# Scores of the later query blocks as plain fp32 products, the two token halves of a block in the two halves of the array's columns

## The chip, the core and the metric

The kernel runs on one core of a Trainium2 chip. The metric is the device time of one execution in microseconds (us). The engines are named as in the profile: PE is TensorE (PEld its weight loads), DVE is VectorE, ACT is ScalarE, POOL is GpSimd, SP is the engine that issues most transfers.

## What is computed

Attention through 49 agents and two feed-forward layers behind it, all in fp32, for 12480 tokens of 128 channels:

```python
a2k = sm(agents, k)              # sm(a, b): softmax of a @ b.T / sqrt(128)
agent_v = a2k @ v                # 49 x 128
q2a = sm(q, agents)              # 12480 x 49: the scores that the change touches
x = q2a @ agent_v
h = np.maximum(x @ w_in, 0.0)    # 128 -> 2048
x = (s * (h * h) + b) @ w_out    # 2048 -> 128
h = np.maximum(x @ w_in2, 0.0)
out = (h * h) @ w_out2
```

## The kernel before

Everything runs on one core with an order written out by hand: within each engine, instructions stand as the Python code issues them. A first part reads keys and values, makes the agents' results and folds them with the first weights into a matrix `M` (49 agents twice, in 128 rows). The main loop then goes over 25 blocks of tokens, 23 of 512 and 2 of 352, in eight steps a block. A step `st` of block `t` issues one pair of 128-row chunks of the first layer up (`up1`, 4 products), of the second layer up for an earlier block (`up2`, 6), and of both layers down (`down`, 6 each). Accuracy is kept by splitting fp32 values into a high and a low part of type float32r: a product is then two or three float32r products that add up in PSUM.

Between these products stands the query work of the next block, one piece at each of some steps: scores (`q_scores` for blocks 0 to 2, `q_scores_T` for the later ones, at step 1), transposing back (`q_back`, step 2), exponential, normalising, and `q_stack`, which makes the block's operand `X`. For blocks from `DIRECT` = 3 on, the queries arrive with channels on the partitions: by a transposing transfer, or every fourth block (`TURN`) by a plain one and a transpose on DVE (`q_turn`, tile `qt`). They are loaded three blocks ahead into three buffers `q_raw`.

For these later blocks the scores work in parts. `q_transpose` copies the queries to a high part `qh` (ACT), `q_low` makes the low part `ql` at the next block's step 0 (DVE). The weights `aS` hold the agents' high parts in columns 0 to 48 and their low parts in columns 64 to 112. `q_scores_T` multiplies low and high queries with `aS`, all 512 tokens at a time, into the PSUM tile `ps_sT`. Two ACT copies and two DVE additions then bring agent high and low rows together into `sT`, where the first 256 tokens of the block lie on partitions 0 to 48 and the second 256 on 64 to 112. `q_back` turns that by two transposes (`ps_b`).

Of the kernel before, what the change touches and what calls it, by code (L numbers as in the profile page):

```python
# [9 lines left out]
F32 = mybir.dt.float32  # L10
F32R = mybir.dt.float32r
# [3 lines left out]
ALU = mybir.AluOpType  # L15
AX = mybir.AxisListType

P = 128
# [15 lines left out]
DIRECT = 3  # L34
# [11 lines left out]
def tile_agent_attention_two_moe(  # L46
# [14 lines left out]
    nc = tc.nc  # L61
    _, N, C = q.shape
    NA = agents.shape[1]
# [4 lines left out]
    GAP = 64  # L68
    KS = GAP + NA
# [13 lines left out]
    blocks, left = [], N  # L83
# [13 lines left out]
    const = ctx.enter_context(tc.tile_pool(name="const", bufs=1))  # L97
    qp = ctx.enter_context(tc.tile_pool(name="qp", bufs=2))
    qs = ctx.enter_context(tc.tile_pool(name="qs", bufs=2))
# [5 lines left out]
    def small(name):  # L105

        flip[0] = (flip[0] + 1) % (flip[1] + 1)
        return ps_m.tile([P, 512], F32, tag=f"m{flip[0]}", name=name)
# [5 lines left out]
    wo2 = [const.tile([P, NCH, C], F32R, name=f"wo2{x}") for x in "hl"]  # L114
    stacks = [const.tile([P, 4, GAP], F32, name=f"stack{i}") for i in range(2)]
    sTs = [const.tile([KS, 256], F32, name=f"sT{i}") for i in range(2)]
    aS = const.tile([P, P], F32R, name="aS")
    av = [const.tile([P, P], F32R, name=f"av{x}") for x in "hl"]
    ones_r = const.tile([P, P], F32R, name="ones_r")
    Xs = [const.tile([P, 512], F32R, name=f"X{i}") for i in range(2)]  # L120
    aT = const.tile([P, GAP], F32, name="aT")
# [1 line left out]
    b_sb = const.tile([P, 1], F32, name="b_sb")  # L123
    y1_bias = const.tile([P, 1], F32, name="y1_bias")
    const.tile([P, 120], F32, name="apart0")
    halves = (0, slice(0, NA)), (1, slice(GAP, KS))

    def split(dst, src, eng_lo, copy=nc.vector.tensor_copy):

# [4 lines left out]
    q_raw, qT, q_sT, q_e, q_st, X = {}, {}, {}, {}, {}, {}  # L134
# [35 lines left out]
    def q_transpose(t):  # L170
        _, p, j = blocks[t]
        n = p * j
        raw = q_raw.pop(t)
        if t < DIRECT:
            ps = small("ps_q")
            for i in range(j):
                nc.tensor.transpose(
                    out=ps[:, i * p:(i + 1) * p], in_=raw[:p, i * C:(i + 1) * C], identity=ident[:p, :p]
                )
            qT[t] = qs.tile([P, 512], F32, tag="qh", name="qT")  # L180
            nc.scalar.copy(qT[t][:, :n], ps[:, :n])
        else:
            hi = qs.tile([P, 512], F32R, tag="qh", name="qh")
            lo = qs.tile([P, 512], F32R, tag="ql", name="ql")
            nc.scalar.copy(hi[:, :n], raw[:, :n])
            qT[t] = (hi, lo, raw)

    def q_low(t):
        _, p, j = blocks[t]
        n = p * j  # L190
        hi, lo, raw = qT[t]
        nc.vector.tensor_tensor(out=lo[:, :n], in0=raw[:, :n], in1=hi[:, :n].bitcast(F32), op=ALU.subtract)

    def q_shift(t, sc):
        _, p, j = blocks[t]
# [16 lines left out]
    def q_scores_T(t):  # L212

        _, p, j = blocks[t]
        n = p * j
        x = qT.pop(t)
        ps = small("ps_sT")
        for z in (1, 0):
            nc.tensor.matmul(out=ps[:, :n], lhsT=aS, rhs=x[z][:, :n], start=(z == 1), stop=(z == 0))  # L219
        sT = sTs[t % 2]  # L220
        for h, to in halves:
            nc.scalar.copy(sT[to, :2 * p], ps[:NA, 2 * p * h:2 * p * (h + 1)])
        for h, to in halves:
            nc.vector.tensor_tensor(
                out=sT[to, :2 * p], in0=ps[GAP:KS, 2 * p * h:2 * p * (h + 1)], in1=sT[to, :2 * p], op=ALU.add
            )
        q_sT[t] = sT

    def q_back(t):
# [9 lines left out]
    def q_exp(t):  # L239
        _, p, j = blocks[t]  # L240
        e = q_e[t]
        nc.scalar.activation(e[:p, :j], e[:p, :j], AF.Exp, scale=SCALE)
# [137 lines left out]
    def finish(n):  # L380

        while undone[0] > n:
            fill(1)

    def m_piece(i):

        sl = slice(i * WC, (i + 1) * WC)
        ps = small("ps_M")
        for z, (x, w) in enumerate(((av[0], wi[1]), (av[1], wi[0]), (av[0], wi[0]))):
            nc.tensor.matmul(out=ps, lhsT=x, rhs=w[:, sl], start=(z == 0), stop=(z == 2))  # L390
        split((M[0][:, sl], M[1][:, sl]), ps, nc.vector, nc.scalar.copy)

    with tc.manual_schedule():

        with tc.tile_pool(name="pre", bufs=1) as pre, tc.tile_pool(name="kp", bufs=2) as kp:
# [23 lines left out]
            nc.gpsimd.memset(aT, 0.0)  # L419
            for x in v_buf:  # L420
                nc.gpsimd.memset(x[:, :, C:], 1.0)
            for x in [aS] + av:
                nc.gpsimd.memset(x.bitcast(F32), 0.0)
            for x in stacks + sTs:
                nc.gpsimd.memset(x, 0.0)
# [9 lines left out]
            ps = small("ps_w")  # L435
            for i in range(16):
                nc.tensor.transpose(out=ps[:, :P], in_=ident, identity=ident)
            ps = small("ps_a")
            nc.tensor.transpose(out=ps[:, :NA], in_=ag, identity=ident[:NA, :NA])
            nc.vector.tensor_copy(aT[:, :NA], ps[:, :NA])  # L440
            nc.vector.tensor_copy(aS[:, :NA], aT[:, :NA])
            nc.vector.tensor_tensor(out=aS[:, GAP:KS], in0=aT[:, :NA], in1=aS[:, :NA].bitcast(F32), op=ALU.subtract)
            mxa = pre.tile([P, 8, NA], F32, name="mxa")

            def k_transpose(g):
# [43 lines left out]
            mxk = pre.tile([P, NA], F32, name="mxk")  # L489
            nc.vector.reduce_max(mxk, mxa.rearrange("p j n -> p n j"), axis=AX.X)  # L490
            q_transpose(0)
            fill(FILL_T)
            ps = small("ps_mt")
# [7 lines left out]
            ps = small("ps_mb")  # L501
# [12 lines left out]
            def set_bias():  # L514
                x = qs.tile([P, 512], F32, tag="ql", name="cs")
                nc.vector.tensor_tensor(
                    out=x.rearrange("p (m c) -> p m c", c=C),
                    in0=ps_cs.rearrange("p (m c) -> p m c", c=C),
                    in1=ident.rearrange("p (m c) -> p m c", m=1).to_broadcast([P, 512 // C, C]),
                    op=ALU.mult,  # L520
                )
                nc.vector.reduce_sum(y1_bias, x, axis=AX.X)
                nc.vector.tensor_mul(y1_bias, y1_bias, b_sb)
# [13 lines left out]
            for g, (_, p, j) in enumerate(kblocks):  # L537
# [6 lines left out]
                for i in range(j):  # L544
                    nc.tensor.matmul(  # L545
                        out=ps_av[:NA, :C + 1],
                        lhsT=S[:p, t0[g] + i],
                        rhs=vs[g][:p, i],
                        start=(g == 0 and i == 0),
                        stop=(g == NG - 1 and i == j - 1),  # L550
# [11 lines left out]
            ps = small("ps_avT")  # L562
# [5 lines left out]
            for c0 in (0, GAP):  # L568
                nc.vector.tensor_tensor(
                    out=av[1][:, c0:c0 + NA], in0=ps[:, :NA], in1=av[0][:, c0:c0 + NA].bitcast(F32), op=ALU.subtract  # L570
# [10 lines left out]
        NB = len(blocks)  # L581
# [12 lines left out]
        def up1(t, i):  # L594
            n = blocks[t][1] * blocks[t][2]
            ps = ps_h.tile([P, 2, 512], F32, tag="h", name="ps_h1")
            for c in range(2):
                sl = slice((2 * i + c) * P, (2 * i + c + 1) * P)
                for z in (1, 0):
                    nc.tensor.matmul(out=ps[:, c, :n], lhsT=M[z][:, sl], rhs=X[t], start=(z == 1), stop=(z == 0))  # L600
            G1[t, i] = hidden(ps, n, 1, nc.scalar.copy if t * NPR + i in HI_ACT else nc.vector.tensor_copy)
# [50 lines left out]
        for st in range(total + L2 + LAG + 1):  # L652
            t, i = divmod(st, NPR)
            if t + 1 < NB and i == QS[2]:
                q_exp(t + 1)
            if st == NPR:
                set_bias()
            for first, left in ((L2, 2 * NW), (L2 + LAG, NW)):
                c, r = divmod(st - first, WC // (2 * P))
                if r == 0 and 0 <= c < NW:  # L660
                    finish(left - 1 - c)
            if st in M_AT:
                m_piece(2 + M_AT.index(st))
            if st < len(FILL_L):
                fill(FILL_L[st])
            if i == 0 and DIRECT <= t + 1 < NB:
                q_low(t + 1)
            if t < NB:
                up1(t, i)
                if i == 0:  # L670
                    for u, far in ((t + 2, t + 2 < DIRECT), (t + 3, DIRECT <= t + 3 < NB)):
                        if far:
                            q_load(u)
                if t + 1 < NB:
                    if t + 2 < NB and i == NPR - 2:
                        q_turn(t + 2)
                    elif t + 2 < NB and i == NPR - 1:
                        q_transpose(t + 2)
                    if i == QS[0]:
                        (q_scores if t + 1 < DIRECT else q_scores_T)(t + 1)  # L680
                    elif i == QS[1] and t + 1 >= DIRECT:
                        q_back(t + 1)
                    elif i == QS[3]:
                        q_norm(t + 1)
                    elif i == QS[4]:
                        q_stack(t + 1)
            t, i = divmod(st - L2, NPR)
            if 0 <= t < NB:
                up2(t, i)
            t, i = divmod(st - LAG, NPR)  # L690
            if 0 <= t < NB:
                down(t, i, wo, G1, py1, "y1")
                if i == NPR - 1:
                    y1_done(t)
            t, i = divmod(st - L2 - LAG, NPR)
            if 0 <= t < NB:
                down(t, i, wo2, G2, py2, "y2")
                if i == NPR - 1:
                    y2_done(t)
# [30 lines left out]
```

## Time and profile before

| what | value |
|---|---|
| median of three runs | 1091.5 us (1089.89 to 1091.57) |
| the profiled execution's own time | 1091.76 us |
| its span, first to last instruction | 1089.8 us |
| PE, DVE, ACT busy in the span | 1073.8, 933.2, 932.9 us |
| mean granted TensorE clock | 0.993 |

The span is what the trace covers; the execution's own time has 2.0 us more around it. Busy time of PE is the time in which at least one matmul record is open; records are longer than the distance between them, since matmuls are pipelined. So the distance of starts tells what a product costs in a row of products.

### The profile page before, as it was taken

The numbers are of one execution on the slowest core, as the hardware profiler recorded it, in microseconds if no ns is written. First come the engines' busy times: TensorE is split into PE (matmuls) and PEld (weight loads), VectorE is DVE, ScalarE is ACT, GpSimd is POOL, SyncE is SP. The second block draws the span as 40 slices with busy tenths as digits, with TensorE's granted clock in tenths as the row PEclk, the third lists the DMA queues.
The fourth block names the chain that finished last, engine by engine and source line by source line (L and its number), as shares of the span: only waits on it lengthen the run. The fifth ranks groups of instructions, "written<-read, shape, count | busy, mean of one in ns | idle before, by whom it ended". The sixth has DMA issues, their size and how long they took to land.

```text
span 1089.8 us, 13795 instructions
## 1 busy us (share of the span) xinstructions
PE 1073.8 (99%) x5105; PEld 903.8 (83%) x5105; DVE 933.2 (86%) x1278; ACT 932.9 (86%) x1081; POOL 12.5 (1%) x36
## 2 busy tenths in 40 slices
PE   9998999999999999999999999999999999999998
PEld 9886788888888888888888888888888888888897
DVE  6888888888888888888888888888888888888876
ACT  6659989889889889889889888888888888888886
POOL 2010000000000000000000000000000000000000
PEclk9899999999999999999999999999999999999999
DMA  9999989992499991499992599991599990000000
GB/s 340 300 173 11 14 4 17 16 8 21 13 8 17 16 7 21 13 7 16 17 7 20 14 7 16 17 7 20 13 8 16 17 5 17 11 2 10 11 10 14
DMA packets 1110795, 34.86 MB, mean 32 GB/s; under 512 B 1092983, under 2 KB 1107144, under 8 KB 1110728
## 3 DMA queue, kind: packets, MB, share of 16 engines
q1 hardware_dynamic: 1107888, 27.58, 99.4%
q0 software_dynamic: 1728, 6.29, 1.8%
q8 instruction: 40, 0.66, 0.4%
q14 instruction: 27, 0.22, 0.1%
q10 hardware_dynamic: 1112, 0.12, 0.1%
HBM read 27.58 MB, written 6.39 MB: 31 GB/s over the span
## 4 chain that ended last, share of the span: by engine, by line
PE 92%; DMA 3%; ACT 1%; DVE 1%; SPq 1%; issue 1%; DVEq 0%
PE ps_y L626 48%; PE ps_h L610 25%; PE ps_h L600 16%; PE ps_av L545 2%; DMA kraw<-in_k_dram 2%; DMA q_raw<-in_q_dram 1%; PE ps_sT L219 1%; SPq L154 1%; ACT r L589 1%; PE ps_x L265 0%; ACT r L590 0%; PE ps_b L234 0%; DVE gl L131 0%; PE ps_cs L512 0%; PE ps_M L390 0%
## 5 line engine op out<-in xcount | busy, mean ns | idle before, releaser
L131 DVE TENSOR_TENSOR gl<-r,gh 128x1024 fp32r<-128x1024 f32 (+2 forms) x402 | 479.8, 1194 | 15.9 <-ACT gh L130 2.3
L589 ACT ACTIVATE r<-ps_h 128x1024 f32<-128x1024 f32 (+2 forms) x402 | 400.4, 996 | 87.7 <-PE ps_h L600 78.3
L590 ACT ACTIVATE r<-r 128x1024 f32<-128x1024 f32 (+2 forms) x402 | 416.5, 1036 | 12.8
L130 DVE CAST gh<-r 128x1024 fp32r<-128x1024 f32 (+1 forms) x397 | 267.4, 674 | 113.6 <-ACT r L590 108.1
L610 PE MATMUL ps_h<-yh,wi2l 128*128 128x512 f32 (+1 forms) x400 | 157.8, 394 | 0.2 <-ACT r L589 0.2
L600 PE MATMUL ps_h<-X,Ml 128*128 128x512 f32 (+1 forms) x400 | 154.1, 385 | 2.1 <-DVE X L276 1.3
L626 PE MATMUL ps_y<-gh,wol 128*128 128x512 f32 (+1 forms) x400 | 154.1, 385 | 1.0 <-ACT y L634 1.0
L626 PE MATMUL ps_y<-gl,woh 128*128 128x512 f32 (+1 forms) x400 | 153.8, 385 | 0.6 <-DVE gl L131 0.6
L600 PE MATMUL ps_h<-X,Mh 128*128 128x512 f32 (+1 forms) x400 | 154.0, 385 | 0.0
L610 PE MATMUL ps_h<-yh,wi2h 128*128 128x512 f32 (+1 forms) x400 | 153.9, 385 | 0.0
L610 PE MATMUL ps_h<-yl,wi2h 128*128 128x512 f32 (+1 forms) x400 | 153.9, 385 | 0.0
L626 PE MATMUL ps_y<-gl,wo2h 128*128 128x512 f32 (+1 forms) x400 | 153.7, 384 | 0.1
L626 PE MATMUL ps_y<-gh,wo2l 128*128 128x512 f32 (+1 forms) x400 | 153.6, 384 | 0.0
L626 PE MATMUL ps_y<-gh,wo2h 128*128 128x512 f32 (+1 forms) x400 | 153.6, 384 | 0.0
L626 PE MATMUL ps_y<-gh,woh 128*128 128x512 f32 (+1 forms) x400 | 153.6, 384 | 0.0
L600 PEld LDWEIGHTS ps_h<-X,Ml 128*128 128x128 f32 x400 | 75.4, 188 | 17.8 <-issue 2.9
L626 PEld LDWEIGHTS ps_y<-gh,wol 128*128 128x128 f32 x400 | 75.3, 188 | 16.3 <-ACT y L634 1.5
L626 PEld LDWEIGHTS ps_y<-gl,woh 128*128 128x128 f32 x400 | 75.3, 188 | 15.7 <-DVE gl L131 1.0
L600 PEld LDWEIGHTS ps_h<-X,Mh 128*128 128x128 f32 x400 | 75.4, 188 | 15.0
L610 PEld LDWEIGHTS ps_h<-yh,wi2h 128*128 128x128 f32 x400 | 75.1, 188 | 14.7
L626 PEld LDWEIGHTS ps_y<-gl,wo2h 128*128 128x128 f32 x400 | 75.2, 188 | 14.5 <-DVE gl L131 0.6
L626 PEld LDWEIGHTS ps_y<-gh,woh 128*128 128x128 f32 x400 | 75.2, 188 | 14.4
(122 smaller groups left out, 887.3 us busy)
## 6 DMA issues: line engine op xcount, KB each, us to landing
kraw<-in_k_dram SPq DMA_DIRECT2D x12, 512.0 KB, 12.0
v<-in_v_dram SPq DMA_DIRECT2D x12, 512.0 KB, 7.9
out_dram<-o SPq DMA_DIRECT2D x92, 64.0 KB, 1.9
q_raw<-in_q_dram SPq DMA_DIRECT2D x18, 256.0 KB, 41.3
raw<-in_moe_w_out_dram POOLq DMA_DIRECT2D x8, 512.0 KB, 7.3
raw<-in_moe_w_in_dram SPq DMA_DIRECT2D x4, 512.0 KB, 7.7
raw<-in_moe_w_in_dram POOLq DMA_DIRECT2D x4, 512.0 KB, 6.9
q_raw<-in_q_dram SPq DMA_DIRECT2D x20, 64.0 KB, 2.3
```

The source lines that it names most:

```text
L130: copy(dst[0], src)
L131: eng_lo.tensor_tensor(out=dst[1], in0=src, in1=dst[0].bitcast(F32), op=ALU.subtract)
L154: nc.sync.dma_start(out=q_raw[t].rearrange("p (j c) -> p j c", c=C)[:p, :j], in_=tokens_of(q, t))
L219: nc.tensor.matmul(out=ps[:, :n], lhsT=aS, rhs=x[z][:, :n], start=(z == 1), stop=(z == 0))
L545: nc.tensor.matmul(out=ps_av[:NA, :C + 1], lhsT=S[:p, t0[g] + i], rhs=vs[g][:p, i], start=(g == 0 and i == 0), stop=(g == NG - 1 and i == ...
L589: nc.scalar.activation(r[:, c, :n], ps[:, c, :n], AF.Relu)
L590: nc.scalar.activation(r[:, c, :n], r[:, c, :n], AF.Square)
L600: nc.tensor.matmul(out=ps[:, c, :n], lhsT=M[z][:, sl], rhs=X[t], start=(z == 1), stop=(z == 0))
L610: nc.tensor.matmul(out=ps[:, c, :n], lhsT=w[:, sl], rhs=y[:, :n], start=(z == 0), stop=(z == 2))
L626: nc.tensor.matmul(out=py[t][:, :n], lhsT=wz[:, m], rhs=g[:, c, :n], start=(m == 0 and z == 0), stop=(m == NCH - 1 and z == 2),)
```

## The change

`q_scores_T` multiplies the fp32 queries as they are, with the fp32 agents `aT` (64 columns, of which 49 are used and the rest zero), in two products of 256 tokens, one per half of the block. The result of the first goes to partitions 0 to 63 of `ps_sT`, that of the second to partitions 64 to 127, so to the lower and the upper half of the array's columns. One ACT copy of 113 partitions brings both into `sT`. The parts `qh`, `ql` and `aS`, with `q_low` and the additions, go.

```diff
@@ const
-    aS = const.tile([P, P], F32R, name="aS")
...
-    halves = (0, slice(0, NA)), (1, slice(GAP, KS))
@@ q_transpose
-            hi = qs.tile([P, 512], F32R, tag="qh", name="qh")
-            lo = qs.tile([P, 512], F32R, tag="ql", name="ql")
-            nc.scalar.copy(hi[:, :n], raw[:, :n])
-            qT[t] = (hi, lo, raw)
-
-    def q_low(t):
-        _, p, j = blocks[t]
-        n = p * j
-        hi, lo, raw = qT[t]
-        nc.vector.tensor_tensor(out=lo[:, :n], in0=raw[:, :n], in1=hi[:, :n].bitcast(F32), op=ALU.subtract)
+            qT[t] = raw
@@ q_scores_T
-        n = p * j
+        n = 2 * p
         x = qT.pop(t)
         ps = small("ps_sT")
-        for z in (1, 0):
-            nc.tensor.matmul(out=ps[:, :n], lhsT=aS, rhs=x[z][:, :n], start=(z == 1), stop=(z == 0))
+        for h in range(2):
+            nc.tensor.matmul(
+                out=ps[GAP * h:GAP * (h + 1), :n], lhsT=aT, rhs=x[:, n * h:n * (h + 1)], start=True, stop=True
+            )
         sT = sTs[t % 2]
-        for h, to in halves:
-            nc.scalar.copy(sT[to, :2 * p], ps[:NA, 2 * p * h:2 * p * (h + 1)])
-        for h, to in halves:
-            nc.vector.tensor_tensor(
-                out=sT[to, :2 * p], in0=ps[GAP:KS, 2 * p * h:2 * p * (h + 1)], in1=sT[to, :2 * p], op=ALU.add
-            )
+        nc.scalar.copy(sT[:, :n], ps[:KS, :n])
@@ first part
-            for x in [aS] + av:
+            for x in av:
...
-            nc.vector.tensor_copy(aS[:, :NA], aT[:, :NA])
-            nc.vector.tensor_tensor(out=aS[:, GAP:KS], in0=aT[:, :NA], in1=aS[:, :NA].bitcast(F32), op=ALU.subtract)
@@ main loop
-            if i == 0 and DIRECT <= t + 1 < NB:
-                q_low(t + 1)
```

On PE, at step 1 of block 2, the scores of block 3 stand between that step's `up1` and `up2`. Before (a row is line, operation, result <- operands, shape of the result):

```order
L600 MATMUL ps_h_1414<-X_90,Ml 128x512
L600 MATMUL ps_h_1414<-X_90,Mh 128x512
L219 MATMUL ps_sT<-ql,aS 128x512
L219 MATMUL ps_sT<-qh,aS 128x512
L610 MATMUL ps_h_1433<-yh,wi2l 128x512
L610 MATMUL ps_h_1433<-yl,wi2h 128x512
```

In the changed kernel the same place on PE reads:

```order
L584 MATMUL ps_h_1406<-X_89,Ml 128x512
L584 MATMUL ps_h_1406<-X_89,Mh 128x512
L208 MATMUL ps_sT<-q_raw,aT 64x256 x2
L594 MATMUL ps_h_1422<-yh,wi2l 128x512
L594 MATMUL ps_h_1422<-yl,wi2h 128x512
```

Two products of 64 rows by 256 columns have taken the place of two of 128 by 512, with the same neighbours; nothing else moves on PE.

On ACT, the copies out of `ps_sT` stand at the end of the same step, between two blocks' hidden activations. Before:

```order
L589 ACTIVATE r<-ps_h_2823 128x1024
L590 ACTIVATE r<-r 128x1024
L222 COPY sT_85<-ps_sT 49x256 x2
L589 ACTIVATE r<-ps_h_2842 128x1024
L590 ACTIVATE r<-r 128x1024
```

In the changed kernel:

```order
L573 ACTIVATE r<-ps_h_2787 128x1024
L574 ACTIVATE r<-r 128x1024
L212 COPY sT_85<-ps_sT 113x256
L573 ACTIVATE r<-ps_h_2803 128x1024
L574 ACTIVATE r<-r 128x1024
```

One copy of 113 partitions stands for two of 49. The cast L185 to `qh`, two steps earlier on ACT, and on DVE the subtraction L192 and the two additions L224 are gone without anything in their place.

## Rows read from the trace of the kernel before

**Rows 1.** The page, part 1: busy time, share of the span, instructions.
```profile
span 1089.8 us, 13795 instructions
...
PE 1073.8 (99%) x5105; PEld 903.8 (83%) x5105; DVE 933.2 (86%) x1278; ACT 932.9 (86%) x1081; POOL 12.5 (1%) x36
```

**Rows 2.** Windows: length, busy time by engine, granted clock (PEclk), DMA share, GB/s.
```profile
core 0: us, PE busy (x) PEld busy (x) DVE busy (x) ACT busy (x) POOL busy (x), PEclk, DMA share, GB/s
75.00:140.00 65.00, 58.14 (x253) 46.35 (x254) 58.91 (x88) 59.75 (x69) 0.00 (x0) 0.97 1.68 11
140.00:1000.00 860.00, 860.00 (x3838) 712.05 (x3837) 747.60 (x956) 759.70 (x846) 0.00 (x0) 1.00 1.07 13
1045.00:1089.80 44.80, 39.99 (x243) 38.94 (x241) 30.71 (x49) 30.61 (x44) 0.00 (x0) 0.98 0.09 15
```

**Rows 3.** Timeline of PE, scores of block 3: start, length (us), line, product.
```profile
139.58 0.39 PE L600 MATMUL ps_h<-X,Mh 128*128 128x512 f32 x1
139.80 0.39 PE L219 MATMUL ps_sT<-ql,aS 128*128 128x512 f32 x1
140.03 0.39 PE L219 MATMUL ps_sT<-qh,aS 128*128 128x512 f32 x1
140.26 0.39 PE L610 MATMUL ps_h<-yh,wi2l 128*128 128x512 f32 x1
...
144.34 0.39 PE L600 MATMUL ps_h<-X,Ml 128*128 128x512 f32 x1
...
145.25 0.36 PE L234 MATMUL ps_b<-ident,sT 113*128 113x113 f32 x2
```

**Rows 4.** Tile ps_sT: count, ns min/median/max, first and last start, forms.
```profile
L222 ACT COPY sT<-ps_sT x44: 281/350/366, 142.0 to 998.5; 49x256 f32<-49x256 f32 x40, 49x176 f32<-49x176 f32 x4
L224 DVE TENSOR_TENSOR sT<-ps_sT,sT x44: 335/422/429, 144.0 to 1000.1; 49x256 f32<-49x256 f32 x40, 49x176 f32<-49x176 f32 x4
...
L219 PE MATMUL ps_sT<-ql,aS x22: 319/389/389, 139.8 to 996.6; 128*128 128x512 f32 x20, 128*128 128x352 f32 x2
```

**Rows 5.** Timeline of PE in the first part: runs of plain fp32 work.
```profile
9.78 1.04 PE L450 MATMUL ps_k<-ident,kraw 128*128 128x128 f32 x8
10.66 1.90 PE L460 MATMUL ps_ks<-aT,kT 128*128 128x64 f32 x16
```

**Rows 6.** Line L545, the agents' values: 98 plain fp32 products.
```profile
L545 PE MATMUL ps_av<-v,S x196: 271/273/454, 46.2 to 70.5; 128*49 128x129 f32 x192, 96*49 96x129 f32 x4
```

**Rows 7.** Timeline of PE, the longest run of L545.
```profile
54.20 16.58 PE L545 MATMUL ps_av<-v,S 128*49 128x129 f32 x148
```

**Rows 8.** Timeline of PE, a narrow window: two transposes between passes of L545.
```profile
53.37 0.49 PE L545 MATMUL ps_av<-v,S 128*49 128x129 f32 x3
53.80 0.47 PE L265 MATMUL ps_x<-ident,stack 128*113 128x128 f32 x2
54.20 0.53 PE L545 MATMUL ps_av<-v,S 128*49 128x129 f32 x3
```

**Rows 9.** Timeline of PE, from L545 to float32r products of 512 columns.
```profile
70.29 0.49 PE L545 MATMUL ps_av<-v,S 96*49 96x129 f32 x3
...
71.05 0.40 PE L512 MATMUL ps_cs<-wol,ones_r 128*128 128x512 f32 x1
```

**Rows 10.** Timeline of PE's weight loads at the same place; in brackets the idle time.
```profile
70.71 0.19 PEld L512 LDWEIGHTS ps_cs<-woh,ones_r 128*128 128x128 f32 x1 [0.19 <-issue]
```

**Rows 11.** Timeline of PE's weight loads, scores of block 3.
```profile
139.58 0.19 PEld L219 LDWEIGHTS ps_sT<-ql,aS 128*128 128x128 f32 x1
```

**Rows 12.** Tile q_raw, columns as in Rows 4.
```profile
L158 SPq DMA_DIRECT2D q_raw<-in_q_dram x16: 633/634/1161, 61.9 to 860.6; - x16
L185 ACT CAST qh<-q_raw x16: 467/604/607, 132.3 to 948.6; 128x512 fp32r<-128x512 f32 x15, 128x352 fp32r<-128x352 f32 x1
L192 DVE TENSOR_TENSOR ql<-q_raw,qh x16: 517/684/687, 136.9 to 953.0; 128x512 fp32r<-128x512 f32 x15, 128x352 fp32r<-128x352 f32 x1
...
L167 DVE STREAM_TRANSPOSE qt<-q_raw x6: 540/704/705, 169.6 to 986.1; 128x512 f32<-128x512 f32 x5, 128x352 f32<-128x352 f32 x1
```

**Rows 13.** The page, part 6: the transposing transfers, KB each, us to landing.
```profile
q_raw<-in_q_dram SPq DMA_DIRECT2D x18, 256.0 KB, 41.3
```

## The prediction, made before the changed kernel was run

> **What bounds the kernel now.** I first read the page's busy times: TensorE (PE) is busy 1073.8 us of a span of 1089.8, VectorE (DVE) and ScalarE (ACT) 933 each [rows 1]. An average over stages does not say where a saving counts, so the table by windows comes next: from 140 us to 1000 us PE is busy in every microsecond and at the full granted clock (1.00, the level of 2.4 GHz), while DVE and ACT have about an eighth of the time free; PE lacks 6.9 us in the window from 75 to 140, and 4.8 us in the last 45 [rows 2].
>
> Busy need not mean useful, since records of matmuls overlap. So the third view is PE's timeline around a changed place. Products of 512 columns start at 139.58 and, 21 later, at 144.34: 4.76 / 21 = 0.2267 us apart, and the two score products of L219 stand in this row at the same distance [rows 3]. From the first L219 at 139.8 to the last at 996.6 lie 21 blocks [rows 4]: about 40.8 us each. A block has 22 x 8 products of the two layers and 2 of scores, 178 x 0.2267 = 40.35, and four transposes, at 0.11 each (a run of eight of 128 columns lasts 1.04 with a last record of 0.27: 0.77 / 7 [rows 5]) 0.44: together 40.79. So nothing is lost to waits: in this stage the kernel is the sum of what PE issues. A slot more or less per block goes into the time in full; work on DVE and ACT does not, as long as they keep up.
>
> **The change, part by part.** It concerns 22 of the 25 blocks (3 to 24), 20 of them of 512 tokens and 2 of 352 [rows 4].
>
> *Removed from PE:* two products of 512 columns, 2 x 0.2267 = 0.4534 us; in the two short blocks two of 352, in proportion 2 x 0.156 = 0.312.
>
> *Added to PE:* two plain fp32 products, each with 64 score columns in the array and 256 tokens passing. How such a product is carried out is seen at L545, also fp32, with 49 score columns in the array: its 98 products have 196 records [rows 6], so each is two passes. A run of 148 passes over 129 columns lasts 16.58, the last record 0.27 [rows 7]: 16.31 / 147 = 0.111 us a pass, 0.86 ns a column. (The fp32r products take 0.2267 / 512 = 0.44 ns: a plain pass costs twice that, and there are two.) A pass of 256 columns is thus 0.220 us, one of 176 is 0.151. There are four passes: end to end 0.881, against 0.4534 removed. What rows of this kernel do not show is whether passes of the two halves, which use different columns of the array and different output partitions, can run beside each other: wherever plain products follow each other here they use the same columns. The bounds are four passes in a row (0.881), and the halves fully side by side (two passes, 0.440).
>
> *The change of shape.* L545 differs from its neighbours in that its results fill fewer than half of the array's columns (128*49), as the new products do; L265 and L512 use more than half. Where three of L545's passes are followed by two transposes and three passes again, the first starts at 53.37 and the last ends at 54.73, so starts at 54.46: 1.09 us, where five distances of 0.111 and two of 0.11 make 0.775. Two crossings, out and in, cost 0.315 [rows 8]. The way out alone: the last L545 starts at 70.29 + 0.49 - 0.27 = 70.51, the second L512 at 71.05, which is 0.54 instead of 0.111 + 0.227: 0.20 [rows 9]; so the way in costs 0.115. The load for the first L512 does not run ahead there: PE's weight loads are 0.19 idle and it starts with its product [rows 9, 10], while in the main loop each load starts with the product before, as that of L219 at 139.58 [rows 3, 11]. The new products lie between products with 128 columns in the array, so each block pays one way in and one out, 0.315. The Trainium skill, "TensorEngine Tiling (Array Packing)", section Key Properties, says that changing the tiling mode, not just the tile, drains the engine; the trace agrees with 0.315 us for two changes, and by that rule nothing is paid between the halves.
>
> *The middle load.* If the second half may start beside the first, its first weights are loaded only when the first half's second pass has begun [rows 11]. A load of 128 columns takes 0.108 (16 passes of L460, too short to cover their loads, last 1.90 less 0.275, over 15 [rows 5]), one of 64 half of that, 0.054.
>
> *Removed from ACT:* the cast L185, 0.604, and one of two copies of 0.350; the one that is left has 113 partitions instead of 49, so it costs between 0.350 and 0.700 (no row has this shape; I take 0.350, since the columns are 256 as before). *From DVE:* L192, 0.684, and two L224 of 0.422 [rows 4, 12]. That is some 0.95 of ACT and 1.53 of DVE a block, on engines that have free time [rows 2]: nothing for the time. If their cover were gone these would be the most they could give, 1.5 x 22 = 34 us, but PE has no gap in that stage to close. The two DVE operations that build aS at about 6 us lie outside it as well; the gaps of PE before 140 and after 1045 us fall into the first blocks and the last layer, where the change has no work. I cost all of this at nothing.
>
> *Waits.* The first pass no longer waits for L192, only for the transfer of the queries or, every fourth block, for DVE's transpose L167, whose first is at 169.6, 11 us ahead of its block's scores (139.8 + 40.8). A raw block is held until the second half is done, 3 us longer (139.8 instead of 136.9), so its buffer's next transfer may start 3 us later. The last transposing transfers are issued at 860.6 and take 41.3, and are read only from 948.6 on [rows 12, 13]: hidden. The transposes L234, at 145.25, now follow a single ACT copy instead of two copies and two additions of 0.422 from 144.0 on [rows 3, 4]: also no wait.
>
> **Sum.** I take the order of the passes as kept, so that only the middle two, the first half's second and the second half's first, can meet: three passes in a row and the middle load. Per full block 3 x 0.220 + 0.054 + 0.315 - 0.4534 = +0.576; per short block 3 x 0.151 + 0.054 + 0.315 - 0.312 = +0.51. 20 x 0.576 + 2 x 0.51 = +12.5 us. The profiled execution's own time is 1091.76 (its span 1089.8 and 2.0 around it), the median of the timed runs 1091.5; on this median the changed kernel takes 1104.0 us, 1.1% more.
>
> **The rivals.**
> A, *no overlap at all*: four passes in a row. 0.881 + 0.315 - 0.4534 = +0.742, short blocks 0.606 + 0.315 - 0.312 = +0.61: 14.8 + 1.2 = +16.0, 1107.5 us. For it: every row of plain products has them one behind the other. Against it: each of these rows has a reason, the same columns.
> The Trainium skill, "TensorE: Matmul & The Clock Gate", section Part 3 on packing small matmuls, has products in different column groups run concurrently, in program order, with 2.38 times the speed measured for three; no run here shows it yet. By the rows alone the price would be A's +16.0, by that rule the sum above, or C if the passes pair up completely.
> C, *halves fully side by side*: two passes, 0.440 + 0.315 - 0.4534 = +0.302, short 0.302 + 0.315 - 0.312 = +0.30: +6.6, 1098.1 us. Against it: the second pass of half 0 stands before both of half 1 in the queue.
> D, *not slower*: the halves side by side and the change of shape hidden, 0.440 - 0.4534 = -0.013 a block: 1091.2 us, no change. It decides only if a block's extra stays under 0.10 us (2.2 / 22), and the 0.315 of the crossings [rows 8] speaks against it. A gain of more than 0.2% would need PE to get shorter: nothing in the profile gives that.
>
> **How the numbers follow.** The main case has 0.47, A 0.31, C 0.14, D 0.05; 0.03 is left for what I have not seen. The range from 1098 to 1109 holds the main case, A with its crossings 0.07 dearer a block than measured, and reaches C, whose value lies on its lower edge. About 0.2% (2.2 us) is what a measurement of this kernel can tell from no change: all cases but D are slower, 0.93; D gives 0.05 for the same; 0.02 is left for faster.
>
> **What the profile after would show.** PE still busy in every microsecond from 140 to 1000. At each place of the scores: four records with 256 columns, two for each half; the start of the third says which case holds: beside or just behind the second (main case, some 0.05 after it), 0.22 after it (A), with the first (C). From the last product before to the first after, some 1.2 us instead of 0.68. The period of a block goes from 40.8 to 41.4 (A 41.6, C 41.1). ACT and DVE lose some 21 and 34 us of busy time, and their idle time before the hidden activations grows. I would be wrong if PE showed gaps in front of the scores (the transfers late), or if the passes took another time a column in the upper half of the array than L545's do in the lower.

## The result and the profile after

The changed kernel takes 1099.69 us (median of six, 1099.21 to 1100.23) against 1091.33 (1089.89 to 1091.65) in the same comparison: ratio 1.0076, 95% interval 1.0066 to 1.0087, so 8.4 us slower, as forecast in sign, with about two thirds of the forecast size.

The page, part 1, and the same windows as before, the last one moved with the span:

```profile
span 1097.8 us, 13770 instructions
...
PE 1082.2 (99%) x5149; PEld 898.4 (82%) x5149; DVE 905.4 (82%) x1210; ACT 915.8 (83%) x1037; POOL 12.3 (1%) x35
```

```profile
75.00:140.00 65.00, 58.30 (x254) 46.17 (x256) 58.96 (x88) 59.63 (x69) 0.00 (x0) 0.97 1.67 11
140.00:1000.00 860.00, 860.00 (x3845) 700.32 (x3842) 714.89 (x885) 736.59 (x795) 0.00 (x0) 1.00 1.07 13
1045.00:1097.00 52.00, 47.99 (x285) 46.20 (x284) 37.65 (x58) 37.47 (x53) 0.00 (x0) 0.99 0.07 13
```

PE is still busy in every microsecond of the main loop at the same granted clock. Over the whole span DVE has 27.8 us less to do and ACT 17.1 [rows 1] (in the window the differences are larger, 32.7 and 23.1 [rows 2], also because a little less of the loop fits into the same 860 us), and the loop is longer all the same: the time is made on PE. The tile `ps_sT`, columns as in rows 4:

```profile
L208 PE MATMUL ps_sT<-q_raw,aT x64: 312/379/430, 139.7 to 963.9; 128*64 128x256 f32 x60, 128*64 128x176 f32 x4
...
L208 PE MATMUL ps_sT<-qt,aT x24: 313/379/431, 180.9 to 1004.5; 128*64 128x256 f32 x20, 128*64 128x176 f32 x4
L212 ACT COPY sT<-ps_sT x22: 284/356/356, 141.9 to 1005.9; 113x256 f32<-113x256 f32 x20, 113x176 f32<-113x176 f32 x2
```

There are 88 records, four for each of 22 blocks. In PE's timeline the first block's scores start at 139.73, the last one's at 1004.30:

```profile
1004.30 0.52 PE L208 MATMUL ps_sT<-qt,aT 128*64 128x176 f32 x4
```

That makes 864.57 / 21 = 41.17 us a block, where it was 40.80 [rows 4]. The 0.37 times 22 are 8.1 us, practically the whole difference. Where they lie is seen in PE's timeline at the place of rows 3:

```profile
139.41 0.39 PE L584 MATMUL ps_h<-X,Mh 128*128 128x512 f32 x1
139.73 0.65 PE L208 MATMUL ps_sT<-q_raw,aT 128*64 128x256 f32 x4
140.32 0.50 PE L594 MATMUL ps_h<-yh,wi2l 128*128 128x512 f32 x1
140.65 0.39 PE L594 MATMUL ps_h<-yl,wi2h 128*128 128x512 f32 x1
...
141.81 0.39 PE L610 MATMUL ps_y<-gh,wol 128*128 128x512 f32 x1
```

Four records fit into 0.65 us. With a last record of 0.38 the last one starts at 140.00, 0.27 after the first; four passes one behind the other would put three distances of 0.22 between them. So the halves run together. Around them every distance is longer than it should be: 0.32 from the last L584 to the first L208 (0.227 between full products), 0.27 from the first passes to the second (0.22), 0.32 from the second passes to L594 (0.22), 0.33 from the first L594 to the second (0.227). PE's weight loads of the same place show what goes with it:

```profile
139.73 0.20 PEld L208 LDWEIGHTS ps_sT<-q_raw,aT 128*64 128x64 f32 x4 [0.35 <-issue]
140.31 0.19 PEld L594 LDWEIGHTS ps_h<-yh,wi2l 128*128 128x128 f32 x1 [0.39 <-issue]
```

Before, each load started with the product ahead of it [rows 11]. Here, at both ends of the visit, the loads stand idle for 0.35 and 0.39 us and start only with their own product, as in rows 10.

### The profile page after: what moved, and what is told of

The parts are those of the page before. It is cut to its first block, busy times and chain, and to the rows that moved or that the text cites. A ratio compares the mean times of both kernels' runs of the same rounds, so it can differ in the third digit from the quotient of the medians.

```text
span 1097.8 us, 13770 instructions
## 1 busy us (share of the span) xinstructions
PE 1082.2 (99%) x5149; PEld 898.4 (82%) x5149; DVE 905.4 (82%) x1210; ACT 915.8 (83%) x1037; POOL 12.3 (1%) x35
## 4 chain that ended last, share of the span: by engine, by line
PE 92%; DMA 3%; ACT 2%; DVE 1%; issue 1%; SPq 0%; DVEq 0%; ACTq 0%
PE ps_y L610 47%; PE ps_h L594 25%; PE ps_h L584 15%; PE ps_av L529 2%; DMA kraw<-in_k_dram 2%; DMA q_raw<-in_q_dram 1%; PE ps_sT L208 1%; ACT r L573 1%; ACT r L574 1%; PE ps_x L251 0%; DVE gl L129 0%; PE ps_b L220 0%; PE ps_cs L496 0%; PE ps_q L175 0%; PE ps_s L198 0%
## 5 line engine op out<-in xcount | busy, mean ns | idle before, releaser
L594 PE MATMUL ps_h<-yh,wi2l 128*128 128x512 f32 (+1 forms) x400 | 160.6, 401 | 0.2 <-ACT r L573 0.2
L584 PE MATMUL ps_h<-X,Ml 128*128 128x512 f32 (+1 forms) x400 | 154.1, 385 | 2.1 <-DVE X L262 1.3
L594 PE MATMUL ps_h<-yh,wi2h 128*128 128x512 f32 (+1 forms) x400 | 154.3, 386 | 0.0
L584 PE MATMUL ps_h<-X,Mh 128*128 128x512 f32 (+1 forms) x400 | 154.1, 385 | 0.0
L594 PE MATMUL ps_h<-yl,wi2h 128*128 128x512 f32 (+1 forms) x400 | 153.9, 385 | 0.0
L594 PEld LDWEIGHTS ps_h<-yh,wi2l 128*128 128x128 f32 x400 | 75.1, 188 | 20.5 <-issue 8.2
L584 PEld LDWEIGHTS ps_h<-X,Ml 128*128 128x128 f32 x400 | 75.2, 188 | 17.8 <-issue 2.9
L584 PEld LDWEIGHTS ps_h<-X,Mh 128*128 128x128 f32 x400 | 75.4, 188 | 14.9
L594 PEld LDWEIGHTS ps_h<-yh,wi2h 128*128 128x128 f32 x400 | 75.1, 188 | 15.2
```

Of the source, the lines that this page charges most:

```text
L594: nc.tensor.matmul(out=ps[:, c, :n], lhsT=w[:, sl], rhs=y[:, :n], start=(z == 0), stop=(z == 2))
```

## The experiments

Two theories stood against each other once this was seen. Theory 1: the halves truly run side by side, and a visit to the half-array shape costs about 0.38 us (0.37 a block, and 0.013 that the two passes are shorter than the two products removed). Theory 2: records that start together prove little, since ends of matmuls are modelled; nothing overlaps, the visit is free, and four passes of 0.21 us are the price. Both give about 0.37 for the changed kernel.

### Both halves in the same columns

```diff
-                out=ps[GAP * h:GAP * (h + 1), :n], lhsT=aT, rhs=x[:, n * h:n * (h + 1)], start=True, stop=True
+                out=ps[:GAP, n * h:n * (h + 1)], lhsT=aT, rhs=x[:, n * h:n * (h + 1)], start=True, stop=True
...
-        nc.scalar.copy(sT[:, :n], ps[:KS, :n])
+        for h, to in (0, slice(0, NA)), (1, slice(GAP, KS)):
+            nc.scalar.copy(sT[to, :n], ps[:NA, n * h:n * (h + 1)])
```

> The changed kernel with both halves' products in the same 64 columns of the array (results side by side on partitions 0 to 63), two ACT copies instead of one. Theory 1 (the halves run side by side in two passes' time, and each visit to the half-array shape costs about 0.38 us): four passes in a row, two more of 0.22 us in each of 20 blocks and of 0.15 in 2, so +9.5 us over the changed kernel, about 1109.2. Theory 2 (the halves never overlap and the visit is free: four passes of about 0.21 are the whole price): no difference, about 1099.7.

Measured: 1110.37 us, ratio to the kernel before 1.0172 (1.0156 to 1.0187). Theory 1 holds, theory 2 falls: with the same passes in the same shape, taking the overlap away costs 10.7 us more. (Columns of the array and output partitions change together here, so the run does not tell which of the two the overlap needs.) The 10.7 are 1.2 more than expected: 0.4 lie ahead of the first scores, which start at 140.09 instead of 139.73, and the last ones start at 1014.29, so a block takes 41.63 us, 0.46 more than in the changed kernel where two passes are 0.43. PE's timeline at a block's scores:

```profile
306.41 0.39 PE L585 MATMUL ps_h<-X,Mh 128*128 128x512 f32 x1
306.73 1.08 PE L208 MATMUL ps_sT<-q_raw,aT 128*64 128x256 f32 x4
307.74 0.50 PE L595 MATMUL ps_h<-yh,wi2l 128*128 128x512 f32 x1
308.08 0.40 PE L595 MATMUL ps_h<-yl,wi2h 128*128 128x512 f32 x1
```

The four records now take 1.08 us instead of 0.65, two passes of 0.215 more, and the distances at the two ends are the ones of the changed kernel (0.32, and 0.34 after the first L595). So two passes of a block had been hidden; if only the middle two had met, as the prediction's main case had it, one would have come back.

### One product of full width

```diff
-        for h in range(2):
-            nc.tensor.matmul(
-                out=ps[GAP * h:GAP * (h + 1), :n], lhsT=aT, rhs=x[:, n * h:n * (h + 1)], start=True, stop=True
-            )
+        nc.tensor.matmul(out=ps[:, :2 * n], lhsT=aT2, rhs=x[:, :2 * n], start=True, stop=True)
...
-        nc.scalar.copy(sT[:, :n], ps[:KS, :n])
+        for h, to in (0, slice(0, NA)), (1, slice(GAP, KS)):
+            nc.scalar.copy(sT[to, :n], ps[to, n * h:n * (h + 1)])
...
```

> The changed kernel with the agents twice, in columns 0 and 64 of full-width plain fp32 weights, one product of all 512 tokens: two passes of 512 columns, no visit to the half-array shape. Theory 1: 2 x 0.44 = 0.88 us instead of 0.453 and nothing else, +0.43 a block on the kernel before, 22 blocks: about +9.3, 1100.6; the third record before and after it at the plain distance. Theory 2: the same sum of passes, 1099.7 to 1100.6; so this run bounds the price of plain passes, and does not tell the two apart.

Measured: 1101.15 us, ratio 1.0088 (1.0071 to 1.0104): +9.9 where 9.3 was expected. PE's timeline at a block's scores:

```profile
304.07 0.39 PE L584 MATMUL ps_h<-X,Mh 128*128 128x512 f32 x1
304.29 1.02 PE L208 MATMUL ps_sT<-q_raw,aT 128*128 128x512 f32 x2
304.75 0.80 PE L594 MATMUL ps_h<-yh,wi2l 128*128 128x512 f32 x1
305.39 0.40 PE L594 MATMUL ps_h<-yl,wi2h 128*128 128x512 f32 x1
```

The first pass starts 0.22 after L584, without a stop. (The first L594's record opens early and is long, so the distance is taken to the second.) From the first pass to the second L594 lie 1.10 us; less one plain distance of 0.227 that is 0.87 for two passes. So a plain pass of 512 columns does cost about 0.44 us, the price a column that L545 had for 129, and without the half shape's overlap the plain scores would cost 0.45 us a block (9.9 / 22) even with no visit. As stated beforehand, this run does not tell the theories apart.

### A tiny product in the half shape, and its control

On the kernel before, ahead of its two score products; the second line is the control's:

```diff
+        nc.tensor.matmul(out=ps[:GAP, :16], lhsT=aT, rhs=x[2][:, :16], start=True, stop=True)
...
+        nc.tensor.matmul(out=ps[:, :16], lhsT=aS.bitcast(F32), rhs=x[2][:, :16], start=True, stop=True)
```

> The kernel before with one plain fp32 product of 16 tokens with the 64 agent columns put ahead of the score products (its result is overwritten by them): all of a visit to the half-array shape, hardly any passing columns. Theory 1: 0.32 to 0.40 us a block, +7 to +9 us on the kernel before, 1098.3 to 1100.3. Theory 2: two short passes, at most 0.06 a block, below 1092.7.

> The control to the tiny product: the same 16 tokens, plain fp32, but with 128 columns of weights, so without a change of shape. Both theories: two passes held back by two weight loads of 0.108, at most 0.2 us a block, and less where loads run ahead: 1091.3 to 1095.7. Theory 1 wants it at least 3 us below the tiny half-shaped product; theory 2 wants it above or equal to it, since its loads are twice as long.

Measured: 1101.76 us for the half shape (ratio 1.0095, 1.0080 to 1.0110) and 1096.70 for the control (1.0046, 1.0031 to 1.0061). The half shape is 5.1 us dearer than the control with weights of half the columns, against theory 2. But both missed their numbers upward: 10.5 us instead of 7 to 9, and 5.4 instead of at most 4.4. The tile's rows, first the half shape, then the control, give 866.5 / 21 = 41.26 and 861.9 / 21 = 41.04 us a block, 0.46 and 0.24 more than before:

```profile
L220 PE MATMUL ps_sT<-ql,aS x22: 427/501/501, 139.4 to 1005.9; 128*128 128x512 f32 x20, 128*128 128x352 f32 x2
```

```profile
L220 PE MATMUL ps_sT<-ql,aS x22: 406/476/476, 138.3 to 1000.2; 128*128 128x512 f32 x20, 128*128 128x352 f32 x2
```

PE's timelines, in the same order:

```profile
304.02 0.39 PE L601 MATMUL ps_h<-X,Mh 128*128 128x512 f32 x1
304.34 0.29 PE L218 MATMUL ps_sT<-q_raw,aT 128*64 128x16 f32 x2
304.56 0.50 PE L220 MATMUL ps_sT<-ql,aS 128*128 128x512 f32 x1
304.90 0.39 PE L220 MATMUL ps_sT<-qh,aS 128*128 128x512 f32 x1
```

```profile
302.20 0.39 PE L601 MATMUL ps_h<-X,Mh 128*128 128x512 f32 x1
302.43 0.29 PE L218 MATMUL ps_sT<-q_raw,aS 128*128 128x16 f32 x2
302.56 0.48 PE L220 MATMUL ps_sT<-ql,aS 128*128 128x512 f32 x1
302.88 0.40 PE L220 MATMUL ps_sT<-qh,aS 128*128 128x512 f32 x1
```

In the control the short passes start on time (0.23), but they are too short to cover the loads of what follows: 0.13 for both, then 0.32 instead of 0.227 to the second L220. Two short passes and the loads that they do not cover thus cost 0.25 us a block (5.4 / 22) with no change of shape. In the half shape the same distance is 0.34, and there is 0.32 on the way in (0.09 too much) and 0.22 over the two short passes (0.13 in the control). The visit is therefore not one cost: by these distances and those of the changed kernel about half of it is the stop at its two borders, 0.09 each, and the rest, as far as the distances tell, loads that cannot run ahead; no run takes one of the two parts away alone.

### Unequal halves

```diff
+            m = n // (1 + h)
             nc.tensor.matmul(
-                out=ps[GAP * h:GAP * (h + 1), :n], lhsT=aT, rhs=x[:, n * h:n * (h + 1)], start=True, stop=True
+                out=ps[GAP * h:GAP * (h + 1), :m], lhsT=aT, rhs=x[:, n * h:n * h + m], start=True, stop=True
             )
...
```

> The changed kernel with the second half's product cut to half of its tokens (128 of 256; a quarter of the later blocks' scores is left out), two ACT copies. The sizes show the order of the four records and what they wait for. Theory 1 with passes taken in turn: 256, 128, 256, 128, the pairs starting together, and the time that of the changed kernel, since the long half sets it. With the order kept half by half, 256, 256, 128, 128: the first short pass beside the second long one.

Measured in one run: 1099.33 us, the changed kernel's time. Line L209 of this kernel at one visit, what has started by 303.60 and what by 303.70:

```profile
L209 PE MATMUL ps_sT<-q_raw,aT x2: 323/376/430, 303.5 to 303.5; 128*64 128x256 f32 x1, 128*64 128x128 f32 x1
```

```profile
L209 PE MATMUL ps_sT<-q_raw,aT x3: 272/323/430, 303.5 to 303.6; 128*64 128x128 f32 x2, 128*64 128x256 f32 x1
```

At 303.5 one long and one short pass start; the next to start, at 303.6, is the second short one, while the first long one still runs and the second long one has not begun. Neither of the two expected orders is this. The halves advance each at its own pace: the short one does not wait for its long neighbour, and the passes of the two do not queue behind each other.

### The relief undone

```diff
+            hi = qs.tile([P, 512], F32R, tag="qh", name="qh")
+            lo = qs.tile([P, 512], F32R, tag="ql", name="ql")
+            nc.scalar.copy(hi[:, :n], raw[:, :n])
             qT[t] = raw
+            parts[t] = (hi, lo, raw)
...
-        nc.scalar.copy(sT[:, :n], ps[:KS, :n])
+        for to in (slice(0, NA), slice(GAP, KS)):
+            nc.scalar.copy(sT[to, :n], ps[to, :n])
+        for to in (slice(0, NA), slice(GAP, KS)):
+            nc.vector.tensor_tensor(out=spare[to, :n], in0=ps[to, :n], in1=sT[to, :n], op=ALU.add)
...
+            if i == 0 and DIRECT <= t + 1 < NB:
+                q_low(t + 1)
```

> The changed kernel with the work that it took off ACT and DVE put back, results unused: the cast of the queries, the subtraction, two copies and two additions of 49 partitions. Theories 1 and 2: that work is covered, 1099.7, within 0.2%. Rival 3 (the relief gave time back, so that the price of the new products on PE is larger than the difference shows): slower, by up to 1.5 us of DVE a block, 33 us at most.

Measured: 1099.33 us, ratio to the kernel before 1.0074 (1.0060 to 1.0087), the changed kernel's own ratio within its interval. The window of the main loop:

```profile
140.00:1000.00 860.00, 860.00 (x3844) 700.40 (x3844) 742.40 (x947) 753.02 (x838) 0.00 (x0) 1.00 1.07 13
```

DVE has 27.5 us more to do there than in the changed kernel, ACT 16.4, and the time is the same. Rival 3 of the expectation falls: what the change takes off ACT and DVE is worth nothing here.

### Two blocks a visit

```diff
...
+        if t in q_sT:
+            return
+        ts = (t, t + 1) if t % 2 == 0 and t + 1 < len(blocks) else (t,)
         ps = small("ps_sT")
+        for u in ts:
+            n, c = 2 * blocks[u][1], 256 * (u - t)
+            x = qT.pop(u) if u == t else q_raw.pop(u)
+            for h in range(2):
+                nc.tensor.matmul(
+                    out=ps[GAP * h:GAP * (h + 1), c:c + n], lhsT=aT, rhs=x[:, n * h:n * (h + 1)], start=True, stop=True
+                )
...
```

> The changed kernel with the scores of two blocks in one visit (blocks 4 and 5, 6 and 7, and so on; the first block and the last alone), into the two halves of one PSUM tile: 12 visits instead of 22, the same passes. Theory 1: ten visits of about 0.38 less, 3.5 to 3.8 us: about 1096. Theory 2: no difference, 1099.7. If the earlier second block waits for its queries, PE shows a gap ahead of L208.

Measured: 1094.91 us, ratio to the kernel before 1.0033 (1.0021 to 1.0046): 4.8 us less than the changed kernel with the same passes, theory 1 again. PE's timeline at a visit, and at the starts of the visits of block 4 and of block 24:

```profile
425.63 0.39 PE L590 MATMUL ps_h<-X,Mh 128*128 128x512 f32 x1
425.95 1.08 PE L213 MATMUL ps_sT<-q_raw,aT 128*64 128x256 f32 x8
426.96 0.50 PE L600 MATMUL ps_h<-yh,wi2l 128*128 128x512 f32 x1
427.30 0.40 PE L600 MATMUL ps_h<-yl,wi2h 128*128 128x512 f32 x1
```

```profile
179.87 0.65 PE L213 MATMUL ps_sT<-qt,aT 128*64 128x256 f32 x4
...
999.50 0.52 PE L213 MATMUL ps_sT<-qt,aT 128*64 128x176 f32 x4
```

Eight records take 1.08 us, as long as four in the same columns did, and the distances at the ends are the same as for four. From block 4 to block 24 lie (999.50 - 179.87) / 20 = 40.98 us a block: of the 0.37 above the kernel before, 0.18 is left, half the visits and half the price. Over 20 blocks that accounts for 3.8 of the 4.8 us; the first scores also start 1.0 us earlier (138.7 instead of 139.7), ahead of any of this, and in the kernels up to here, which leave the work ahead of it practically alone, that start lies anywhere between 138.1 and 140.1. Differences of one or two us between kernels can come from there.

### The overlap where the kernel already has the half shape

On the kernel before, for its products of S and v (L545), with the two sums added at the end:

```diff
-                        out=ps_av[:NA, :C + 1],
+                        out=ps_av[GAP * h:GAP * h + NA, :C + 1],
...
+            av2 = pre.tile([NA, C + 1], F32, name="av2")
+            nc.scalar.copy(av2, ps_av[GAP:KS, :C + 1])
...
+            nc.vector.tensor_tensor(out=av2, in0=ps_av[:NA, :C + 1], in1=av2, op=ALU.add)
```

where `h` is `i % 2`; a second kernel also takes one decoding step less behind each group and gives the steps back in the main loop:

```diff
-FILL_V = (3,) * 7 + (2,) * 5 + (0,)
+FILL_V = (2,) * 7 + (1,) * 5 + (0,)
...
-FILL_L = (2,) * 22
+FILL_L = (3,) * 12 + (2,) * 10
```

> The kernel before, scores in parts as they were, with the 98 products of L545 (49 columns, in the half-array shape already) put by turns into the two halves of the array's columns, two sums that one ACT copy and one DVE addition bring together. Theory 1 (two streams run side by side): the passes of L545 take half of their 21.8 us, so PE waits for DVE there instead; DVE's row of work up to the last shift of S ends at 66 us where the last product stood at 70.5, so 3 to 4 us less, 0.5 to 1 of it given back for the addition: 2 to 3.5 us faster, about 1088.5. Theory 2: no overlap, 1091.5 to 1092.5.

> The same with one decoding step less on DVE behind each of those products' groups (12 steps, moved to the first steps of the main loop), so that DVE reaches the shifts of S sooner. Theory 1: up to 6 us (12 steps of 0.5) more in this stage, if the main loop's start has room for them; DVE is busy 59 of 65 us there, so part of it is lost again: between 1084 and 1089. Theory 2: no gain, 1091 to 1094.

Measured: 1090.91 us, ratio 0.9994 (0.9983 to 1.0005), no difference to be told; and 1093.97 with fewer decoding steps, ratio 1.0019 (1.0008 to 1.0031), slower. The overlap is there, the gain is not. PE's timeline and, from the table of waits of 45 to 75 us, what PE waits for:

```profile
49.67 1.97 PE L546 MATMUL ps_av<-v,S 128*49 128x129 f32 x32
51.88 1.09 PE L546 MATMUL ps_av<-v,S 128*49 128x129 f32 x16 [0.23 <-ACT S L529]
...
57.64 1.21 PE L546 MATMUL ps_av<-v,S 128*49 128x129 f32 x16 [2.92 <-ACT S L529]
...
66.60 0.43 PE L546 MATMUL ps_av<-v,S 96*49 96x129 f32 x4 [0.93 <-DMA v<-in_v_dram]
```

```profile
ACT S L529 <- DVE S L528: 8.6, 8, 2.2
...
PE ps_av L546 <- ACT S L529: 5.3, 6, 2.9
```

32 passes take 1.97 us, (1.97 - 0.27) / 15 = 0.113 for two, where one took 0.111 [rows 7]. But then PE waits 5.3 us for the exponentials, whose inputs stand behind DVE's decoding. The last L546 ends at 67.03 instead of 70.78 [rows 9]; of these 3.7 us the medians show 0.5, less than their uncertainty. The runs give a hint where some of it goes: the mean granted clock lies between 0.987 and 0.994 in the twelve runs of this kernel, and the time follows it. The three at 0.993 or more take 1089.2 to 1090.0 us, the two at 0.987 take 1094.0 and 1094.3; the kernel before has 0.992 to 0.994 in 22 of 23 runs. In which stretch the clock is lower was not traced. With the decoding moved, the main loop's start pays for it; the window from 75 to 100, first of the kernel before, then with fewer decoding steps:

```profile
75.00:100.00 25.00, 20.63 (x87) 16.13 (x88) 22.19 (x39) 22.45 (x28) 0.00 (x0) 0.93 1.86 8
```

```profile
75.00:100.00 25.00, 18.25 (x64) 13.36 (x64) 21.12 (x37) 20.99 (x27) 0.65 (x1) 0.86 1.73 30
```

PE is busy 2.4 us less there, at a lower granted clock (0.86 of full speed against 0.93), and the first scores of block 3 start at 141.4 instead of 139.8. Neither is a version that beats the kernel before.

## Why the prediction was right, and where it was off

*What bounds the kernel:* right. PE was the sum of what it issues, and the difference is 22 times one block's, to 0.3 us. Relief of ACT and DVE at nothing: right, and shown by the relief undone. Its size was put too high, 21 and 34 us where the page shows 17.1 and 27.8: durations of records were added up, and records of neighbouring operations overlap (by 0.07 before the first L224 at 144.03, whose forerunner runs from 142.88 for 1.22), which explains most of it. The one copy left on ACT costs 0.356 (0.350 taken, 0.700 feared); no wait appeared ahead of the scores, the idle time there being the loads'.

*Two passes a half at 0.22 us:* right; 0.215 by the kernel with eight records (1.08 - 0.38 = 0.70 over three distances, the first of them 0.27: 0.43 / 2).

*The step that failed:* "I take the order of the passes as kept, so that only the middle two ... can meet: three passes in a row and the middle load." The halves run fully side by side, two passes and no load between the halves: a block's four loads take 0.20 us together, and with the halves in the same columns two passes of 0.215 come on top, not one. That is rival C, which had 0.14 and 1098.1 us. Its counterargument, that the second pass of half 0 stands before both of half 1 in the queue, was no reason: the unequal halves show that passes in different columns do not wait for each other. With C's overlap the sum falls from +12.5 to +6.6.

The Trainium skill, "TensorE: Matmul & The Clock Gate", section Part 3, had it right that products in different column groups run concurrently; the kernel with both halves in the same columns shows it at 10.7 us. Its addition that they keep the program order in their starts is not borne out by the unequal halves, where passes of the two halves start in neither order.

*The term that was mis-sized:* the two crossings, 0.315 us from a place where transposes stand between. At the scores a visit costs 0.38 (0.37 + 0.013). The distances at the scores give most of it: 0.09 on the way in, 0.05 between first and second passes, 0.09 on the way out, 0.11 for the next load, and some 0.03 more over the five products behind it (140.65 to 141.81 is 1.16 instead of 1.13). This last part lay outside the stretch of rows 8. 22 x 0.07 = 1.5 us: 6.6 + 1.5 = 8.1, against 8.4 measured. The period of a block, 41.17, is next to C's 41.1 (A's own sum gives 41.5, not the 41.6 written).

So the forecast of 1104.0 was 4.3 us too high: one error of 5.9 us upward in the overlap, one of 1.5 downward in the crossing. That 1099.69 still lies in the range is in part luck: the range reached down to C, a case with a chance of 0.14, and the second error took back a quarter of the first. Rivals A and D are excluded for the changed kernel: A was built, and takes 1110.37 us; D wanted a free crossing, and the visits counted in the kernel with two blocks each are not free.

## What to carry to other kernels

Two products with at most 64 result columns each, put into the two halves of the array's columns, run in the time of one here (plain fp32, 256 or 129 columns passing through); but on a TensorE that is already full every visit to that shape costs 0.38 us in this loop, so make few visits with much work in each: here a block's scores gain 0.013 us by the shape and lose 0.38 by the visit. Work taken off engines that are not the bound gave nothing back (27.5 us of DVE's and 16.4 of ACT's, put back, cost nothing): look first for an engine that is busy in every microsecond of the stage, and count only what the change does to that one. Where the overlap does shorten a stage, ask what feeds it next.

## What the runs showed of the hardware that was not expected

Passes in different halves of the array's columns advance independently: with 256 and 128 columns the short half's second pass started at 303.6, before the long half's second. And a product too short to cover the next weight load is dear even without any change of shape: 16 columns of plain fp32 at full width cost 0.25 us a block.
